# A linear-attention and MLP block on one core: float32r projections and sums rewritten as float16 pairs with scales found on the chip

## The chip, the cores and the metric

The kernel runs on one NeuronCore of one Trainium2 chip. The time is that of the device, in microseconds; lower is better. Three runs of the kernel before took 1063.47, 1063.88 and 1066.28 us, so its time is 1063.88 us. The traced execution, to which every number of the trace belongs, took 1062.19 us; its instructions span 1060.5 us of that.

## The reference

All tensors are float32, with 2048 tokens (S), width D = 576, 32 heads of 18 and an MLP width of 4608. What is computed, in the order of the reference:

```
mod = silu(c) @ w_mod                     # six vectors of 576: sa, ca, ga, sb, cb, gb
h   = layernorm(x) * (1 + ca) + sa
q, k, v = split(h @ wqkv)                 # three projections, 576 x 576 each
phi(t) = where(t > 0, t + 1, exp(t)) + 1e-6
kv  = sum over tokens of phi(k)^T v ;  z = sum over tokens of phi(k)      # per head
o   = (phi(q) @ kv) / (phi(q) @ z + 1e-6)
x   = x + ga * (o @ wo)
h   = layernorm(x) * (1 + cb) + sb
x   = x + gb * (silu(h @ w1) @ w2)
```

## The kernel before

Tokens are cut into 16 tiles of 128 and 4 blocks of 512. The program has three stages that overlap at their seams.

**Stage A**, up to about 200 us of the span, is attention without its output. The normalised and modulated input is transposed, and held as `hT`: per 128-row chunk of D (four and a half chunks, the half one doubled up) a high part rounded to float32r and a low part, the rest. The weights of q and k are split the same way (`w_hi`, `w_lo`; names `wq` and, for k, the tiles `w` and `v`). A projection of one tile is then 14 products for each half of 288 columns: for a whole chunk high x high, high x low and low x high, for the half chunk two. Lines L548 (the first two k tiles), L873 (`project`) and L400 (`x_passes`, used for the last five q tiles, and for the attention output, whose operands were float16 pairs already) issue them. Behind a k projection come `phi` (`phi_steps`: exp on ScalarE, the positive part on ScalarE or VectorE, their sum on VectorE), a split of phi(k) into high and low (`pk`), and `zsum` on GpSimd. v is never projected: the kernel sums phi(k) times normalised x over the tokens (`sum_steps`, L998, five sums of 24 or 16 products per block, from the split rows `xs` and `pk`), and multiplies the sums by the modulation and by the weight of v once at the end (L1171).

**The start** loads x tiles 0 and 1, the first third of w_mod, then the k weights (five chunks, the last in two halves), and the q weights. `mods` are multiplied by silu(c) and summed on VectorE (L583, L586, L593), turned into columns by small TensorE products (L522), and `add_cols` (L526) makes `cols["a"]`: the shift and 1 + scale of each row of `hT`. For each chunk k ScalarE then makes the high part of the k weight (L477) and of `hT` (L607), VectorE and GpSimd the low parts (L482, L372, L272), and the 56 products of tiles 0 and 1 run (L548). While TensorE has nothing to do, `keep_busy` (L542) issues products of ones that nobody reads.

**The middle**, from 200 to about 355 us, makes the attention output, the second layer norm, and the MLP of the first group of 256 columns. **The MLP**, from about 355 us to the end, is float16 pairs throughout, with products of 128x512 (L1947) and 128x288 (L2031).

The order of instructions on each engine is fixed, in two ways. For the last two thirds a planner (`Schedule.emit`) lists them by due times worked out from costs in the code; for everything before that, a table of numbers (`ORDERS`, one list per engine) replaces the order in which the code was written. An engine takes its instructions strictly in that order: one that waits holds up all behind it. Loads are issued by SyncE (SP) in its own order; a load takes one of eight semaphores, so that SyncE stands at a load until an earlier one has landed.

## Time and profile before

| | us |
|---|---|
| median of three runs | 1063.88 |
| traced execution, its own time | 1062.19 |
| its span | 1060.5 |
| TensorE busy | 1048.6 (99%) |
| VectorE busy | 867.0 (82%) |
| ScalarE busy | 718.5 (68%) |
| GpSimd busy | 741.8 (70%) |
| TensorE without work, in all | 11.9 |

A row of the groups names the line, engine and operation, the tiles written and read, the shapes and the count; behind the bar stand the busy time of the group, the mean time of one, and the idle time of the engine just before them. A matmul's own time (296 ns for a float32r one of 288 columns) overlaps its neighbours'; what one costs is the distance from start to start. "fp32r" and "f32" operands of matmuls in stage A are float32r. In a row of the timeline the first number is the start in us from the span's start, the second how long the group lasted.

### The profile page before, as it was taken

The page shows a single profiled execution, that of the slowest core. Times are in us where ns is not written, and L with a number is a line of the kernel's source. Part 1 is how long each engine was busy: PE and PEld are TensorE (multiplying, and loading weights), DVE is VectorE, ACT ScalarE, POOL GpSimd, SP SyncE. Part 2 cuts the span into 40 slices and gives each one's busy share as a digit, 9 for nine tenths or more (in the row PEclk, how much of TensorE's full clock was granted, in tenths as well). Part 3 has the DMA queues.
Part 4 walks back from the last instruction along what each step waited for, and adds up shares of the span by engine and source line. Part 5 has one row for each costly group of instructions (what it writes and reads, how often), then busy time and mean ns, then how long its engine had stood idle before and what let it go on. Part 6 is the DMA issues. An engine that isn't in the chain of part 4 may idle for free.

```text
span 1060.5 us, 19049 instructions
## 1 busy us (share of the span) xinstructions
PE 1048.6 (99%) x7001; PEld 740.5 (70%) x7001; DVE 867.0 (82%) x1439; ACT 718.5 (68%) x1342; POOL 741.8 (70%) x809
## 2 busy tenths in 40 slices
PE   9999999999999999999999999999999999999998
PEld 9999999887775555666666666666666666666665
DVE  6777675789989898898987888978977977898767
ACT  6875484368667876776865876767757766766554
POOL 3656536566843788899797688876876878787463
PEclk9999999999999999999999999999999999999999
DMA  8596970495657785588478566667567567526422
GB/s 301 159 204 197 155 191 8 104 209 133 185 175 249 241 255 187 179 292 209 125 259 211 175 223 220 172 219 215 183 209 204 185 216 223 187 90 203 152 80 113
DMA packets 139246, 198.75 MB, mean 187 GB/s; under 512 B 63820, under 2 KB 96464, under 8 KB 139152
## 3 DMA queue, kind: packets, MB, share of 16 engines
q1 hardware_dynamic: 106340, 196.35, 61.1%
q10 hardware_dynamic: 32812, 1.18, 3.1%
q8 instruction: 55, 0.90, 0.4%
q14 instruction: 39, 0.32, 0.1%
HBM read 176.77 MB, written 15.48 MB: 181 GB/s over the span
## 4 chain that ended last, share of the span: by engine, by line
PE 92%; DMA 3%; DVE 2%; ACT 1%; SPq 1%; issue 0%; ACTq 0%; DVEq 0%
PE up L1947 33%; PE down L2031 32%; PE psK L873 9%; PE big L400 6%; PE psG L998 5%; PE small L1452 2%; PE big L1463 1%; PE psK L1210 1%; DMA hT<-hd 1%; DMA xt<-in_A_x_dram 1%; PE small L385 1%; DMA acc<-in_A_wqkv_dram 1%; PE down L2065 1%; PE up L2065 1%; PE psG L1171 0%; DMA hd<-S 0%
## 5 line engine op out<-in xcount | busy, mean ns | idle before, releaser
L1947 PE MATMUL up<-hT,w 128*128 128x512 f16 x1264 | 319.2, 379 | 2.2 <-DMA hT<-hd 2.2
L1947 PEld LDWEIGHTS <-w 128*128 128x128 f16 x1492 | 145.7, 98 | 135.3 <-issue 4.6
L2040 DVE SCALAR_TENSOR_TENSOR acc<-acc,set,down 128x576 f32<-128x576 f32 x128 | 103.5, 810 | 34.6 <-PE down L2031 33.6
L1965 ACT ACTIVATE f<-f,set 128x512 f32<-128x512 f32 x102 | 73.3, 719 | 62.6 <-DVE f L1971 52.6
L1985 POOL TENSOR_TENSOR s<-f,f 128x256 f32<-128x256 f32 x66 | 54.4, 825 | 73.3 <-ACT f L1966 70.9
L2031 PE MATMUL down<-w,hc 128*128 128x288 f16 x600 | 91.5, 286 | 0.0
L2031 PE MATMUL down<-w,hb 128*128 128x288 f16 x600 | 90.8, 286 | 0.0
L2031 PE MATMUL down<-w,hT 128*128 128x288 f16 x480 | 82.8, 286 | 0.4 <-DVE acc L2044 0.4
L1969 DVE TENSOR_TENSOR f<-up,p 128x512 f32<-128x512 f32 x102 | 69.5, 683 | 16.4 <-PE up L1947 8.2
L1966 ACT ACTIVATE f<-f,set 128x512 f32<-128x512 f32 x102 | 73.6, 722 | 3.3
L2031 PEld LDWEIGHTS <-hc 128*128 128x128 f16 x600 | 58.7, 98 | 23.1
L2031 PEld LDWEIGHTS <-hb 128*128 128x128 f16 x600 | 58.7, 98 | 22.2 <-issue 0.2
L2009 POOL TENSOR_TENSOR hc<-s,hc 128x512 f16<-128x512 f32 x50 | 63.6, 1272 | 8.2 <-ACT hc L2005 8.2
L1971 DVE TENSOR_TENSOR f<-up,f 128x512 f32<-128x512 f32 x68 | 46.8, 688 | 24.9 <-PE up L1947 24.1
L400 PE MATMUL big<-w,qT 128*128 128x288 f16 x448 | 65.4, 286 | 1.2 <-DMA qT<-w 1.2
L1989 POOL TENSOR_TENSOR f<-f,s 128x256 f32<-128x256 f32 x66 | 53.8, 815 | 18.1 <-DVE hb L2009 10.2
L2031 PEld LDWEIGHTS <-hT 128*128 128x128 f16 x480 | 47.0, 98 | 26.6 <-issue 0.8
L1982 POOL TENSOR_TENSOR s<-f 128x256 f32<-128x256 f32 x66 | 57.3, 869 | 5.6 <-ACT f L1962 4.3
L1987 POOL TENSOR_TENSOR s<-s,f 128x256 f32<-128x256 f32 x66 | 55.9, 847 | 3.5
L2031 PE MATMUL down<-w,ha 128*128 128x288 f16 x396 | 56.6, 286 | 0.0
L2031 PE MATMUL down<-w,hd 128*128 128x288 f16 x396 | 56.0, 286 | 0.0
L2009 POOL TENSOR_TENSOR hd<-s,hd 128x256 f16<-128x256 f32 x66 | 49.0, 742 | 7.0 <-ACT hd L2005 6.9
(424 smaller groups left out, 2767.2 us busy)
## 6 DMA issues: line engine op xcount, KB each, us to landing
hT<-hd SPq DMA_DIRECT2D x101, 640.0 KB, 4.3
hT<-hd SPq DMA_DIRECT2D x65, 512.0 KB, 4.3
hT<-in_B_w_dram SPq DMA_DIRECT2D x14, 576.0 KB, 5.5
hT<-in_B_w_dram SPq DMA_DIRECT2D x28, 256.0 KB, 7.5
raw<-in_B_w_dram SPq DMA_DIRECT2D x11, 576.0 KB, 5.7
v<-in_B_w_dram SPq DMA_DIRECT2D x9, 576.0 KB, 5.1
acc<-in_A_x_dram SPq DMA_DIRECT2D x16, 288.0 KB, 3.5
raw<-in_B_w_dram SPq DMA_DIRECT2D x9, 512.0 KB, 5.7
```

The source lines that it names most:

```text
L400: T.matmul(ps, xpart(a), wpart(b), start=n == 0, stop=n == len(XW) - 1)
L873: T.matmul(o, part(a), w(b), start=c == 0 and m == 0, stop=c == KC and m == 1)
L1947: T.matmul(ps, left, right, start=first and m == 0, stop=m == len(seq) - 1, skip_group_check=True)
L1965: A.activation(f, f, AF.Silu, scale=factor(self.g, "inv"))
L1966: A.activation(f, f, AF.Identity, scale=factor(self.g, "delta"))
L1969: V.tensor_add(f, self.bank[bank[1]], self.p1)
L1982: G.tensor_sub(self.s3, half(i, 0, 0), half(i, 0, 1))
L1985: G.tensor_add(self.s[:, 0:1], half(i, 0, 1), half(i, 1, 1))
L1987: G.tensor_sub(self.s[:, 1:2], self.s[:, 0:1], half(i, 0, 0))
L2009: eng.tensor_sub(t[:, :, 1, :], src, t[:, :, 0, :])
L2031: T.matmul(ps[:, p, :HALF], left[:, u, p * P : (p + 1) * P], right[:, v], start=n in (1, 5, 7, 6) and j == 0, stop=j == len(passes) - 1, s ...
L2040: V.scalar_tensor_tensor(dst, dst, factor(self.g, "ratio"), ps[:, :, :HALF], op0=ALU.mult, op1=ALU.add)
```

## The change

It does six things.

1. **Float16 pairs in stage A.** `hT`, the k and q weights, `xs` and `pk` become pairs of float16 values: a high part, and the rest rounded to float16. The number of products, their shapes and the passes stay the same. Since a pair takes half the room, `hT` exists four times over and not twice, `pk` and `xs` eight times and not four.
2. **Powers of two, found on the chip.** Float16 needs values of a fit size, so every operand gets a factor. `ETA` (for `hT`) comes from the squares of the first third of w_mod, summed on ScalarE, and of silu(c); `SIZE_K` from the largest absolute value of each row of the k weight (five VectorE reductions); `SIZE_Q` from the squares of the q weight (five ScalarE squares); `SIGMA` (for `pk`) from the modulation columns and the k weight. Each is summed over the partitions by a small TensorE product with ones, and turned into a power of two by a chain of VectorE operations on single columns (`find_size`, `sigma_steps`). `add_cols` needs `ETA`, the split of the k weight `SIZE_K`, that of the q weight `SIZE_Q`, that of phi(k) `SIGMA`.
3. **Features in the projection's scale.** phi's exp takes its scale and bias from these factors; the positive part is one VectorE operation for every tile (`relu_of`: before, ScalarE did it for 12 of the 16 k tiles and the last five q tiles); the features stay multiplied by the factor, which z and the denominators take out.
4. **Low parts.** On VectorE a low part is one operation that scales and subtracts; on GpSimd it is two (scale in place, then subtract). For 9 of the k tiles ScalarE scales phi(k) once more ahead of GpSimd's subtraction.
5. **Orders.** All five lists of `ORDERS` are new, so the start, stage A, the middle and the entry of the MLP run in another order.
6. In the last unit of the MLP, the low part of `hb1` is now listed behind the last update of `U` of its block.

The diff, without the lists of `ORDERS` and the places that only rename:

```diff
-            0-24 27-29 25-26 30-44 47 49 51 53 55 57-58 45-46 48 50 59-62 52 54 63-66 69-70 56 73-74 67-68 71-72 75-76
...
-    hT = [hTa.tile([P, 2 * KC + 2, 512], F32R, name="hT")]
+    def pair_of_hT():
+        t = hTa.tile([P, 2 * KC + 2, 512], F32, name="hT")
+        y = t.rearrange("p n t -> p (n t)").bitcast(F16)
+        return [y[:, 512 * (2 * KC + 2) * i : 512 * (2 * KC + 2) * (i + 1)].rearrange("p (n t) -> p n t", t=512) for i in range(2)]
...
     def w_hi(wpart, k, full):
-        return A.copy(wpart(k if k < KC else 2 * KC), full)
+        return A.activation(wpart(k if k < KC else 2 * KC), full, AF.Identity, scale=size_of(wpart))
...
+        by, h = size_of(wpart), slice(0, P) if k < KC else slice(64, P)
+        hi, lo = (wpart(k), wpart(KC + k)) if k < KC else (wpart(2 * KC)[h],) * 2
+        if eng is V:
+            return V.scalar_tensor_tensor(lo, full[h], by[h], hi, op0=ALU.mult, op1=ALU.subtract)
+        G.tensor_mul(full[h], full[h], by[h].to_broadcast([h.stop - h.start, D]))
+        return G.tensor_sub(lo, full[h], hi)
+
+    def scale_bits(q):
+        V.tensor_scalar(q.bitcast(I32), q.bitcast(I32), 1, 0x3F800000, op0=ALU.logical_shift_right, op1=ALU.bitwise_and)
+
+    def find_size(rows, spot, size, inv, by):
+        t, q = both_sizes[:, 0:1], both_sizes[:, 1:2]
+        V.tensor_reduce(t, rows, axis=AX.X, op=ALU.add)
+        T.matmul(psT()[:, spot : spot + 1], ones, t, start=True, stop=True, skip_group_check=True)
+        V.tensor_scalar(q, psT()[:, spot : spot + 1], 2.0**-80, None, op0=ALU.max)
+        scale_bits(q)
+        V.reciprocal(size, q)
+        V.tensor_scalar(size, size, 2.0**-50, None, op0=ALU.mult)
...
+    def exp_of(e, ps, inv, by):
+        return A.activation(halves(e), ps[:, :, :HALF], AF.Exp, bias=by[2], scale=inv)
+
+    def relu_of(a, ps, by):
+        return V.tensor_scalar(halves(a), ps[:, :, :HALF], by[1], by[1], op0=ALU.add, op1=ALU.max)
...
     def add_cols(k0, k1):
         src = colps[:, 2 * k0 : 2 * k1]
-        V.tensor_add(cols["a"][:, k0:k1, :], src.rearrange("p (k a) -> p k a", a=2), plus1.unsqueeze(1).to_broadcast([P, k1 - k0, 2]))
+        V.scalar_tensor_tensor(cols["a"][:, k0:k1, :], src.rearrange("p (k a) -> p k a", a=2), ETA,
+                               plus_h.unsqueeze(1).to_broadcast([P, k1 - k0, 2]), op0=ALU.mult, op1=ALU.add)
...
+    for k in range(KC):
+        A.activation(room, mods[k][:, :, :D], AF.Square, accum_out=rows_m[:, k : k + 1])
+    A.activation(room[:, 0], tmod[:, :D], AF.Square, accum_out=rows_m[:, KC : KC + 1])
...
+    V.tensor_reduce(half_of[:, 0:1], rows_m, axis=AX.X, op=ALU.add)
+    T.matmul(psT()[:, 64:66], ones, half_of[:, 0:2], start=True, stop=True, skip_group_check=True)
...
+    for k in START:
+        V.tensor_reduce(rows2[:, k : k + 1], acc[k], axis=AX.X, op=ALU.max, apply_absolute_value=True)
+    V.scalar_tensor_tensor(rows2, rows2, float(D), rows2, op0=ALU.mult, op1=ALU.mult)
+    find_size(rows2, 66, SIZE_K, INV_K, BY_K)
...
+    for k in START:
+        A.activation(e_, acc[5 + k], AF.Square, accum_out=rows_q[:, k : k + 1])
+    find_size(rows_q, 67, SIZE_Q, INV_Q, BY_Q)
...
+        phi_steps(ps, k, a, [an], INV_K, BY_K)
+        do("POOL", 1.53, lambda: G.tensor_add(zsum, zsum, a) if t else G.tensor_copy(zsum, a), [an], ["zsum"])
+        do("ACT", 0.68, lambda: A.activation(hi, a, AF.Identity, scale=SIGMA), [an, "sigma"], [f"pkh{i}"])
+        if t in BY_POOL:
+            do("ACT", 0.68, lambda: A.activation(a, a, AF.Identity, scale=SIGMA), [], [an])
+            do("POOL", 1.5, lambda: G.tensor_sub(lo, a, hi), [an, f"pkh{i}"], [f"pkl{i}"])
         else:
-            do("DVE", 1.2, lambda: V.tensor_sub(lo, a, f32(hi)), [an, f"pkh{i}"], [f"pkl{i}"])
+            do("DVE", 1.2, lambda: V.scalar_tensor_tensor(lo, a, SIGMA, hi, op0=ALU.mult, op1=ALU.subtract), [an, f"pkh{i}", "sigma"], [f"pkl{i}"])
+    def sigma_steps():
+        ps, g = psT()[:, 0:3], "G1"
...
+        do("DVE", 0.4, terms, [], ["some"])
+        pe(0.25, lambda: T.matmul(ps, ones, t3, start=True, stop=True, skip_group_check=True), ["some"], [g])
```

**What moves.** First, SyncE's loads at the start. `xt` is x, `hT` at this place w_mod (its room is used for `hT` later), `acc_91` and the first `acc_92` the k weight. Before, and then as changed:

```order
L437 DMA xt<-in_A_x_dram 128x576 x2
L468 DMA tmod<-in_w_mod_dram 64x576 x2
L460 DMA hT<-in_w_mod_dram 128x2x576 x2
L407 DMA acc_92<-in_A_wqkv_dram 64x576
L460 DMA hT<-in_w_mod_dram 128x2x576 x2
L404 DMA acc_91<-in_A_wqkv_dram 128x576
L406 DMA acc_92<-in_A_wqkv_dram 64x576
L437 DMA xt<-in_A_x_dram 128x576
L404 DMA acc_91<-in_A_wqkv_dram 128x576
L437 DMA xt<-in_A_x_dram 128x576
L404 DMA acc_91<-in_A_wqkv_dram 128x576 x2
```

```order
L457 DMA xt<-in_A_x_dram 128x576 x2
L480 DMA hT<-in_w_mod_dram 128x2x576
L488 DMA tmod<-in_w_mod_dram 64x576 x2
L480 DMA hT<-in_w_mod_dram 128x2x576
L427 DMA acc_92<-in_A_wqkv_dram 64x576
L480 DMA hT<-in_w_mod_dram 128x2x576
L424 DMA acc_91<-in_A_wqkv_dram 128x576
L426 DMA acc_92<-in_A_wqkv_dram 64x576
L480 DMA hT<-in_w_mod_dram 128x2x576
L424 DMA acc_91<-in_A_wqkv_dram 128x576 x3
L457 DMA xt<-in_A_x_dram 128x576 x2
```

The last chunk of the k weight was the 16th load and is the 14th, ahead of x tiles 2 and 3; the last of w_mod has a whole chunk and two halves of the k weight ahead of it, where it had half a chunk.

Second, ScalarE from the first high part of the k weight on, before and as changed. L477 and L500 are the high parts of weights, L607 and L669 those of `hT`, L680 the squares of the q weight, L362 and L382 the normalising of x:

```order
L477 CAST w<-acc_91 128x576
L594 COPY hT<-hT 128x64
L607 ACTIVATE hT<-psK,col_a 128x256
L477 CAST v<-acc_92 128x576
L629 CAST xs_112<-xt 128x576
L607 ACTIVATE hT<-psK,col_a 128x256
...
L607 ACTIVATE hT<-psG_117,col_a 128x256
L607 ACTIVATE hT<-psG_116,col_a 128x256
L477 CAST w<-acc_91 128x576
L477 CAST wq<-acc_93 128x576
```

```order
L500 ACTIVATE w<-acc_92,crow 128x576
L655 COPY hT<-hT 128x64
L669 ACTIVATE hT<-psK,col_a 128x256
L500 ACTIVATE w<-acc_91,crow 128x576 x4
L680 ACTIVATE e,crow<-acc_92 128x576 x2
...
L669 ACTIVATE hT<-psG_124,col_a 128x256
L680 ACTIVATE e,crow<-acc_93 128x576
L669 ACTIVATE hT<-psG_123,col_a 128x256
L1008 CAST xs_115<-xt 128x576
L500 ACTIVATE wq<-acc_92,crow 128x576 x3
```

The rows left out in the second piece are L669 twice, L680, L382 for x tiles 2 and 3 (two of 64 columns, two of 576) and one cast of x. The five squares and the normalising now stand among the five high parts of `hT`, ahead of the first high part of the q weight.

Third, TensorE from the first k products to the first q products. L590 is L548 of before, L938 is L873, L584 is L542 (`keep_busy`); L517 is the product of `find_size`, L981 that of `sigma_steps`, L1357 the transposing of x tiles 2 and 3. Before, and then as changed:

```order
L548 MATMUL psK<-w,hT 128x288 x2
L542 MATMUL psG_117<-ones 128x128
...
L548 MATMUL psK<-v,hT 128x288 x4
L1269 MATMUL psG_116<-ident,xt 128x128
L873 MATMUL psK<-wq,hT 128x288 x2
```

```order
L584 MATMUL psG_124<-ones 128x128 x14
L590 LDWEIGHTS hT
L590 MATMUL psK<-w,hT 128x288
...
L584 MATMUL psG_124<-ones 128x128 x3
L517 MATMUL psG_124<-crow,ones 128x1
...
L981 MATMUL psG_124<-crow,ones 128x3
...
L1357 MATMUL psG_124<-ident,xt 128x128 x2
L938 MATMUL psK<-wq,hT 128x288
```

Of the 56 k products of tiles 0 and 1, ten stand ahead of L517 (the one for `SIZE_Q`; that for `SIZE_K` stands further up), 24 and eight transposes between L517 and L981, 22 and two transposes behind L981. None of these small products was there before.

459 lines of the change are left out of this document (247 added, 212 removed).

## The prediction

> **What bounds the kernel now.** I read the page's busy times and its chain first.
>
> ```profile
> PE 1048.6 (99%) x7001; PEld 740.5 (70%) x7001; DVE 867.0 (82%) x1439; ACT 718.5 (68%) x1342; POOL 741.8 (70%) x809
> PE 92%; DMA 3%; DVE 2%; ACT 1%; SPq 1%; issue 0%; ACTq 0%; DVEq 0%
> ```
>
> TensorE works in 1048.6 of 1060.5 us, and the chain that ends last is TensorE for 92%. So two things count: what a product costs, and how long TensorE stands. The windows tell where it stands (columns: stretch, length, busy time and count of PE, PEld, DVE, ACT, POOL, then granted clock, DMA share, GB/s).
>
> ```profile
> 0.00:20.00 20.00, 18.01 (x134) 17.52 (x135) 11.53 (x35) 10.11 (x21) 5.65 (x11) 1.00 0.92 316
> 20.00:40.00 20.00, 19.86 (x152) 19.52 (x151) 19.44 (x47) 18.78 (x35) 8.80 (x10) 1.00 0.55 174
> 40.00:160.00 120.00, 120.00 (x905) 120.00 (x904) 83.14 (x138) 79.18 (x121) 69.49 (x51) 1.00 0.88 186
> 200.00:220.00 20.00, 18.76 (x147) 16.07 (x146) 17.42 (x31) 9.63 (x15) 13.22 (x13) 1.00 0.86 189
> 320.00:340.00 20.00, 18.81 (x109) 10.13 (x107) 18.16 (x33) 13.93 (x26) 2.93 (x4) 1.00 0.76 258
> 340.00:360.00 20.00, 17.29 (x95) 9.18 (x95) 16.48 (x26) 16.21 (x35) 18.88 (x26) 1.00 0.78 240
> ```
>
> Stage A, from 40 to 160 us, is full; VectorE and ScalarE are at 69% and 66% there. Idle are the seams: 1.2 us after 200, 1.2 + 2.7 us between 320 and 360.
>
> **The gain: the pace of a product.** Stage A's 905 products in 120 us come one every 132.6 ns. Float16 products of the same 288 columns run at the end of this kernel:
>
> ```profile
> 1045.62 0.53 PE L2065 MATMUL down<-w,hb 128*128 128x288 f16 x3
> 1045.99 0.53 PE L2065 MATMUL down<-w2B,hc 128*128 128x288 f16 x3
> ...
> 1054.81 0.53 PE L2065 MATMUL down<-w2B,hc 128*128 128x288 f16 x3
> ```
>
> 75 products (25 rows of three) take 9.19 us: 122.5 ns each, 10.1 less. The products that the change turns to float16:
>
> ```profile
> L998 PE MATMUL psG<-w,xs 128*128 128x288 f32 x336 | 53.3, 296 | 0.0
> L873 PE MATMUL psK<-w,hT 128*128 128x288 f32 x308 | 48.6, 296 | 0.0
> L873 PE MATMUL psK<-wq,hT 128*128 128x288 f32 x264 | 41.9, 296 | 0.0
> L873 PE MATMUL psK<-v,hT 128*128 128x288 f32 x128 | 24.4, 295 | 0.0
> L400 PE MATMUL big<-wq,hT 128*128 128x288 f32 x120 | 21.7, 313 | 0.0
> L998 PE MATMUL psG<-w,v 128*128 128x288 f32 x112 | 20.2, 296 | 0.0
> L548 PE MATMUL psK<-w,hT 128*128 128x288 f32 x44 | 7.2, 304 | 0.0
> L400 PE MATMUL big<-v,hT 128*128 128x288 f32 x20 | 3.8, 303 | 0.0
> L548 PE MATMUL psK<-v,hT 128*128 128x288 f32 x12 | 2.2, 307 | 0.0
> ```
>
> These are 1344. The 56 of L548 belong to the start, counted below; the other 1288 give 1288 x 10.1 = **13.0 us**. Bounds: 0 if float16 is no quicker here, 13.0 if all of it comes through.
>
> **The loss: the start.** How far is the first q product put off? Before it stands here, after the 56 k products:
>
> ```profile
> 28.59 0.51 PE L873 MATMUL psK<-wq,hT 128*128 128x288 f32 x2
> ```
>
> Now I follow the new order. `SIZE_K` needs the whole k weight. Its last load is now the 14th; the 14th of before was issued and landed so:
>
> ```profile
> 10.41 0.33 SPq L437 DMA_DIRECT2D xt<-in_A_x_dram x1
> DMA to landing us min/median/max: 6.9/6.9/6.9
> ```
>
> So the weight is there at 10.4 + 6.9 = 17.3 us. The last of w_mod, which VectorE met at 13.9 (first row below), has 0.44 MB more ahead of it: at 316 GB/s 1.4 us, so 15.3; ScalarE's last squares end near 17.7. Prices of single operations:
>
> ```profile
> 13.91 0.95 DVE L593 SCALAR_TENSOR_TENSOR hT<-hT,sc 128x256 f32<-128x256 f32 x2 [0.25 <-DMA hT<-in_w_mod_dram]
> L711 DVE TENSOR_REDUCE crow<-bc_gb 128x1 f32<-128x576 f32 x2 | 1.5, 744 | 0.0
> L691 DVE TENSOR_SCALAR crow<-crow 128x4 f32<-128x4 f32 x1 | 0.2, 170 | 0.0
> 20.51 1.02 ACT L607 ACTIVATE hT<-psG,col_a 128x256 fp32r<-128x256 f32 x2
> 21.42 0.67 ACT L477 CAST w<-acc 128x576 fp32r<-128x576 f32 x1
> L674 ACT ACTIVATE hT<-hT 128x1152 f32<-128x1152 f32 x14 | 16.2, 1158 | 0.0
> L674 ACT ACTIVATE hT<-hT 128x256 f32<-128x256 f32 x7 | 2.9, 414 | 0.0
> L674 ACT ACTIVATION_READ_ACCUMULATOR hT<-hT 128x1 f32 x35 | 6.6, 187 | 0.0
> L362 ACT ACTIVATE xt<-xt,mv 128x576 f32<-128x576 f32 x3 | 2.6, 868 | 0.1
> L362 ACT ACTIVATE xt<-xt,mv 128x64 f32<-128x64 f32 x3 | 1.3, 439 | 2.1 <-DVE mv L356 2.1
> ```
>
> - The last largest value (a reduction of 576, 0.74) ends about 18.6: another reduction and a piece of `mods` stand close ahead of it. Behind it VectorE has three short operations, a piece of `mods` (0.48) and seven steps of `find_size` and of `ETA`: with 0.15 to 0.17 each, `SIZE_K` at 20.6. The first high part of a weight was made at 14.75 before.
> - Eight more VectorE operations, 1.6 us, stand ahead of the first `add_cols`, for which ScalarE's first high part of `hT` waits: 22.2. Behind it wait four high parts of weights and all else.
> - ScalarE then has, up to the last square of the q weight, four pieces of `hT`, four high parts of weights, a cast, five squares and four normalisings. Two pieces of `hT` take 0.91 between starts (20.51, 21.42), 0.46 each; a high part takes 0.67, the cast 0.57 where the next operation starts before it ends; a square of 576 lies between the rows of 256 and 1152 at 0.68, with the read of 187 that follows it 0.87; the normalisings 0.1 less than their rows, 0.34 and 0.77. Sum: 4 x 0.46 + 4 x 0.67 + 0.57 + 5 x 0.87 + 2 x 0.34 + 2 x 0.77 = **11.7**. So the squares are done at 33.9.
> - On TensorE only ten k products stand ahead of the second product of L517. It issues in order, so it does those ten and stands until the squares are summed (a short VectorE operation and a handover each way, 0.6): 34.5. Of the 46 others, 24 and eight transposes follow (3.8 us, 38.3). Then L981 waits for `SIGMA`: after the squares VectorE has the seven steps of `SIZE_Q` (35.9), two low parts of `hT` (0.7), two of weights (0.72 each, which wait for ScalarE's high parts until 36.6) and the short steps of `SIGMA`, to 39.1. The remaining 22 and two transposes (2.9) end at **42.0**.
>
> That is 42.0 - 28.6 = **13.4 us**. This term is the least sure: 8.5 if loads and chains overlap better, 20 if they don't (below).
>
> **Smaller terms.** The first projections afterwards find ScalarE and VectorE behind: the first q tile waits for a PSUM buffer that exp and the positive part free (0.7), the next for an exp queued behind two rows of w_mod (1.3). Both are worked out with TensorE as late as above; if it is later still, they vanish. Between 0 and 2.0 I take **1.0**. Moved to VectorE are 17 positive parts, about 0.75 each, 13 us over 160: it goes from 69% to 77%, still below TensorE. The additional scaling on ScalarE (9 of 0.57) fits into its 34%, and the two GpSimd operations of a low part into what `pk`'s eight buffers allow. These I cost at nothing; if VectorE were late with the low part of `pk`, sums would stop, one stall of 0.7 per block. The seams have new orders. Their idle time was 5.1 us; without a row that tells which way they go I take 0, with 3 either way. The move of `hb1`'s low part, in the last microseconds of the MLP, lies between 0 and 0.4.
>
> **Sum.** -13.0 + 13.4 + 1.0 = +1.4: the traced execution's 1062.2 becomes 1063.6. The median of the runs, 1063.9, is 1.7 above that execution, so the forecast is **1065.3 us**. A difference of 0.3%, 3.2 us, is about what can be told from no change; this is within it.
>
> **Rivals.**
>
> - *The start costs 8.5* (0.28). If the operations of the start overlap better than in order and price, `SIZE_K` comes at 19 (1.6 earlier), the eight operations behind it take 1.0, and ScalarE's 17 overlap by 0.1 more each (10.0), then the squares end at 30. If the wait for `SIGMA` (0.8) is covered too, the first q product starts at 42.0 - 3.9 - 0.8, near 37. For it: ScalarE was idle half of the first 20 us (10.11). Against: in 20 to 40 us it was busy 18.78 of 20. Time: -13.0 + 8.5 + 0.5 = -4.0, 1059.9. It decides if the second L517 comes ahead of 31 us.
> - *The short operations are slow* (0.24). Late in this kernel the same short operation is four times as long:
>
> ```profile
> L691 DVE TENSOR_SCALAR raw<-raw 128x4 f32<-128x4 f32 x7 | 4.9, 698 | 0.2
> L695 DVE TENSOR_SCALAR set<-set 128x4 f32<-128x4 f32 x9 | 4.0, 441 | 0.2
> L482 POOL TENSOR_TENSOR w<-acc,w 128x576 fp32r<-128x576 f32 x2 | 3.1, 1536 | 8.1 <-ACT w L477 8.1
> ```
>
> With 170 alone and 698 beside GpSimd's work, one that waits costs 0.53 more. GpSimd's low parts of k (1.5 us, and now two operations each) run just when the seven steps of `SIZE_Q` and the ten of `SIGMA` do. If 13 of the 17 are caught, 6.9 us more: 1072. Against: GpSimd was busy 8.8 of the 20 us, so fewer may be caught. It decides from about 4 of them on. The Trainium skill, page "SBUF — State Buffer", section "🔬 SBUF: two separate sides", says that a port pair shared by VectorE and GpSimd is locked for a whole instruction by whichever starts first; that is a reason for rows of 698 and speaks against this change. By that rule all 17 steps could be held, an estimate of 17 x 0.53 = 9.0 us more.
> - *TensorE comes back slowly* (0.06). It stands some 10 us ahead of the second L517; nothing in the trace of before stands so long, and its windows show a granted clock of 1.00 throughout. If the 3.8 us of products behind it ran at half pace, they would end at 42.1, past the 39.1 of `SIGMA`: 3.0 later, 1068.3. The Trainium skill, page "TensorE: Matmul & The Clock Gate", section "What's actually happening", gives such a rule: half the clock after an idle window, until about 3.4 us of work are done. By its figure the loss is an estimate of 1.7 us; no run here shows it.
> - *Float16 gains nothing in stage A* (0.04): 1065.3 + 13.0 = 1078. Against it stands the pace of L2065.
>
> **How the numbers follow.** The forecast has 0.38 and its own range is 1062 to 1068.5, from the seams' 3 us. With 0.28 at 1056 to 1062, 0.24 at 1068 to 1075, and 0.10 for the last two, 8 in 10 lie from **1056.5** to **1073.5**. Faster than 1060.7 is most of the first rival and little of the forecast: 0.28. Slower than 1067.1 is the second, the fourth, the third and a slice of the forecast: 0.34. Within: 0.38.
>
> **What would show it.** Rows of stage A at 122 ns from start to start; a stretch of some 10 us ahead of the second L517 in which TensorE has nothing; that product at 34 to 35, the first q product near 42 us. TensorE's busy time falls by some 13 us, its idle time rises by as much. A second L517 ahead of 31 proves the start's term wrong; idle time at 200 to 360 us away from 5 the seams'; windows of stage A with TensorE under 99% the cover that I gave VectorE.

## The result and the profile after

| | before | after |
|---|---|---|
| median of the runs, us | 1063.81 (1063.47 to 1066.28) | 1072.37 (1071.13 to 1074.08) |
| ratio, with its 95% interval | | 1.0087 (1.0066 to 1.0108) |
| traced execution, its own time | 1062.19 | 1071.29 |
| its span | 1060.5 | 1069.4 |
| first q product starts | 28.59 | 47.52 |
| first product of `x_passes` | 199.67 | 210.96 |
| last 128x512 product of the MLP | 1041.4 | 1050.7 |

The changed kernel is 8.6 us slower. (Of the kernels below, e1_sizes_known has one run of 1215.15 us at a mean granted clock of 0.845, and its median is that of its four other runs.) The page of its traced execution opens with the busy times; the second row quoted is the chain of waits by engine.

```profile
PE 1042.4 (97%) x6999; PEld 698.5 (65%) x6999; DVE 901.8 (84%) x1495; ACT 726.4 (68%) x1350; POOL 753.2 (70%) x818
PE 81%; DVE 12%; DMA 3%; issue 1%; ACT 1%; SPq 1%; POOL 0%; DVEq 0%; ACTq 0%; POOLq 0%
```

TensorE works 6.2 us less, in a span that is 8.9 longer. Of the chain, 12% is VectorE's now, where it was 2%. The windows of the changed kernel (columns as before: stretch, length, busy time of PE, PEld, DVE, ACT, POOL, granted clock, DMA share, GB/s) tell where that is.

```profile
0.00:20.00 20.00, 12.57 (x69) 11.42 (x69) 10.31 (x23) 11.84 (x23) 4.95 (x11) 0.80 0.91 260
20.00:40.00 20.00, 13.65 (x78) 12.73 (x78) 19.16 (x69) 12.91 (x27) 10.49 (x9) 0.69 0.43 140
40.00:60.00 20.00, 17.50 (x140) 13.50 (x138) 18.40 (x41) 18.38 (x29) 12.48 (x10) 1.00 0.58 169
60.00:80.00 20.00, 17.86 (x144) 13.81 (x142) 19.53 (x28) 16.56 (x24) 14.90 (x11) 1.00 1.01 250
80.00:100.00 20.00, 19.44 (x158) 15.08 (x157) 19.53 (x25) 14.73 (x21) 13.97 (x9) 1.00 1.02 147
40.00:160.00 120.00, 114.79 (x927) 90.13 (x925) 103.84 (x166) 91.76 (x134) 71.87 (x50) 1.00 0.87 184
```

Up to 40 us TensorE has 147 instructions where it had 286. VectorE is at work for 92 to 98% of each slice from 20 to 100 us. The granted clock is under 1.00 in the first 40. In 40 to 160 us there are 927 products although TensorE stands for 5.2 us: they come faster. TensorE's own timeline shows the start (start, length, group, and in brackets the idle time ahead of it and what ended it):

```profile
28.56 5.17 PE L584 MATMUL psG<-ones 128*128 128x128 f32 x28
33.57 0.41 PE L590 MATMUL psK<-w,hT 128*128 128x288 f16 x2
37.47 1.15 PE L590 MATMUL psK<-w,hT 128*128 128x288 f16 x8 [3.49 <-DVE raw L392]
38.46 0.83 PE L584 MATMUL psG<-ones 128*128 128x128 f32 x6
39.12 0.28 PE L517 MATMUL psG<-crow,ones 128*128 128x1 f32 x2
43.99 0.38 PE L981 MATMUL psG<-crow,ones 128*128 128x3 f32 x2 [0.66 <-DVE crow L978]
47.52 0.65 PE L938 MATMUL psK<-wq,hT 128*128 128x288 f16 x4 [0.20 <-DVE a L533]
```

The second product of L517, for `SIZE_Q`, comes at 39.12, that for `SIGMA` (L981) at 43.99. Ahead of both TensorE stood 3.49 us for VectorE's L392, which reads the transposed x out of PSUM, multiplies and shifts it, and so frees the buffer that the next k products write.

From the landmarks in the table the span's 8.9 us come apart: the first q product +18.9; from there to `x_passes` -7.6 (163.4 us in place of 171.1); from there to the last 128x512 product -2.0; the end -0.4. In the 163.4 us TensorE stands 4.3, before it stood 0.25. So the work there went from 170.8 to 159.1 us, by 11.7.

### The profile page after: what moved, and what is told of

The parts are those of the page before. It is cut to its first block, busy times and chain, and to the rows that moved or that the text cites. A ratio compares the mean times of both kernels' runs of the same rounds, so it can differ in the third digit from the quotient of the medians.

```text
span 1069.4 us, 19132 instructions
## 1 busy us (share of the span) xinstructions
PE 1042.4 (97%) x6999; PEld 698.5 (65%) x6999; DVE 901.8 (84%) x1495; ACT 726.4 (68%) x1350; POOL 753.2 (70%) x818
## 3 DMA queue, kind: packets, MB, share of 16 engines
q10 hardware_dynamic: 32812, 1.18, 3.0%
## 4 chain that ended last, share of the span: by engine, by line
PE 81%; DVE 12%; DMA 3%; issue 1%; ACT 1%; SPq 1%; POOL 0%; DVEq 0%; ACTq 0%; POOLq 0%
PE up L2035 34%; PE down L2119 31%; PE psK L938 6%; PE psG L1087 5%; PE big L1551 1%; DVE st L367 1%; PE big L420 1%; DMA acc<-in_A_wqkv_dram 1%; PE small L1540 1%; DVE pn L810 1%; DVE hT L276 1%; DVE acc L1479 1%; DMA tmod<-in_w_mod_dram 1%; DMA hT<-hd 1%; PE down L2153 1%
## 5 line engine op out<-in xcount | busy, mean ns | idle before, releaser
L938 PEld LDWEIGHTS <-hT 128*128 128x128 f16 x700 | 68.2, 98 | 21.2 <-issue 2.8
L2119 PEld LDWEIGHTS <-hc 128*128 128x128 f16 x600 | 58.7, 98 | 22.2 <-issue 0.5
L1087 PE MATMUL psG<-w,xs 128*128 128x288 f16 x448 | 64.6, 286 | 1.9 <-DVE w L966 1.5
L2119 PEld LDWEIGHTS <-hT 128*128 128x128 f16 x480 | 47.0, 98 | 26.1 <-issue 0.3
```

Of the source, the lines that this page charges most:

```text
L938: T.matmul(o, part(a), w(b), start=c == 0 and m == 0, stop=c == KC and m == 1)
L1087: T.matmul(ps[:, h, :HALF], l, pk[pp[t]][:, u, h * HALF : (h + 1) * HALF], start=t == 0 and m == 0, stop=t == 3 and m == len(left) - 1)
L2119: T.matmul(ps[:, p, :HALF], left[:, u, p * P : (p + 1) * P], right[:, v], start=n in (1, 5, 7, 6) and j == 0, stop=j == len(passes) - 1, s ...
```

## The experiments

The first eight kernels take one suspected part out of the changed kernel, or move it. Then the change is built up from the kernel before. Ratios are to the kernel before, run beside each; the first q product is that of the traced execution.

| run | what it is | median, us | ratio (95%) | first q product |
|---|---|---|---|---|
| after | the change | 1072.37 | 1.0087 (1.0066 to 1.0108) | 47.52 |
| e1_sizes_known | sizes as constants | 1070.76 | 1.0071 (1.0044 to 1.0097) | 44.18 |
| e2_no_pool_lows | GpSimd's low parts of k left out | 1071.13 | 1.0068 (1.0044 to 1.0093) | 46.29 |
| e5_stats_later | statistics moved back on VectorE | 1073.14 | 1.0092 (1.0063 to 1.0121) | 46.63 |
| e3_no_mod_sums | a sum on GpSimd left out | 1072.31 | 1.0068 (1.0046 to 1.0090) | 47.77 |
| e4_fillers | TensorE kept at work | 1073.70 | 1.0083 (1.0067 to 1.0100) | 47.99 |
| e7_relu_scalar | eight positive parts on ScalarE | 1075.60 | 1.0096 (1.0067 to 1.0126) | 46.86 |
| e8_known_ordered | e1 in an order of its own | 1071.38 | 1.0060 (1.0042 to 1.0079) | 42.86 |
| e10_mod_loads_first | w_mod loaded earlier | 1072.10 | 1.0079 (1.0057 to 1.0101) | 48.64 |
| e6_sums_alone | before, only the sums float16 | 1060.79 | 0.9973 (0.9958 to 0.9987) | 32.90 |
| e9_before_f16 | before, all pairs float16, no factor | 1054.84 | 0.9915 (0.9897 to 0.9933) | 30.84 |
| e11_find_k | e9 and the keys' size found | 1073.96 | 1.0080 (1.0058 to 1.0102) | 46.97 |
| e12_features_scaled | e9 and the features' new form | 1068.68 | 1.0031 (1.0012 to 1.0051) | 33.29 |

### e1_sizes_known: are the operations of finding the loss?

```diff
+    for to, value in ((SIGMA, 2.0**-7), (UNDO, 2.0), (ETA, 4.0), (UNDO_H, 0.25), (SIZE_K, 16.0), (SIZE_Q, 64.0), (INV_K, 2.0**-6),
...
+        added("DVE", 0, V.memset(to, value))
-    for k in range(KC):
-        A.activation(room, mods[k][:, :, :D], AF.Square, accum_out=rows_m[:, k : k + 1])
...
+    def find_size(pe_):
+        skip("DVE", "PE", *["DVE"] * 9)
```

In this and the next kernels `added` puts an instruction behind a place of an engine's list, and `skip` leaves the place of one empty; all others keep theirs. The squares, the largest values, both size chains and that of `SIGMA` are gone.

> The changed kernel with ETA, SIZE_K, SIZE_Q, SIGMA and what follows from them as constants, written once at the start: the ten squares on ScalarE, the five largest values and all steps of find_size and sigma_steps on VectorE, and their four products are left out (the constants are the powers of two that these inputs give). Theory A (the pace of float16 came through in full, and the loss is the finding at the start): the first q product, at 47.5 us in the changed kernel, comes at 30 to 34; the execution takes 1052 to 1056. Theory B (float16 pairs lose something later as well, in stage A's VectorE work or at the seams): the start recovers, but the time stays at 1060 or more.

The first q product comes 3.3 us earlier, and the time is 1.6 lower, less than the intervals can tell from nothing. Theory A missed both numbers, and the start that theory B expected to recover didn't. So the operations of finding are 3.3 of the start's 18.9 us while their order stays. Even of these only 1.9 are left at the first product of `x_passes` (209.08). The timeline of TensorE shows the same picture as the changed kernel's, shifted:

```profile
25.35 5.11 PE L596 MATMUL psG<-ones 128*128 128x128 f32 x28
30.30 0.41 PE L602 MATMUL psK<-w,hT 128*128 128x288 f16 x2
34.27 1.15 PE L602 MATMUL psK<-w,hT 128*128 128x288 f16 x8 [3.56 <-DVE raw L419]
```

The sizes are there at once, yet TensorE still waits 3.56 us for the same step: VectorE's list has other work ahead of it.

### e2_no_pool_lows: are short operations slow beside GpSimd?

```diff
+        if wpart is wkp:
+            skip("Pool", "Pool")
+            return added("Activation", 29, A.activation(lo, full[h], AF.Identity, scale=by[h]))
```

This leaves six GpSimd operations out; the low parts of the k weights then hold a copy, so this part of the result is not computed.

> The changed kernel; GpSimd's six operations for the low parts of three chunks of the k weight are left out, and ScalarE writes a copy in their place (no low part, so these chunks have a wrong one). Theory A (VectorE's queue bounds the start, and it is stretched by operations that wait beside GpSimd): VectorE's operations of 1.1 us between 28 and 36 us go back to 0.15 to 0.8, the second L517 comes 3 us earlier (36), the first q product too, and the time falls by 2 to 4 us, to 1068 to 1070. Rival (ScalarE's chain of squares bounds it, as forecast): three more operations stand in that chain, L517 is later by 0 to 2 us, and the time is the same or 2 us longer.

Here are five short operations of the changed kernel in the groups of 20 to 48 us:

```profile
L376 DVE SCALAR_TENSOR_TENSOR mv<-mv 128x2 f32<-128x2 f32 x1 | 1.2, 1183 | 0.0
L975 DVE TENSOR_TENSOR crow<-crow 128x5 f32<-128x5 f32 x1 | 1.1, 1122 | 0.0
L986 DVE SCALAR_TENSOR_TENSOR crow<-crow 128x1 f32<-128x1 f32 x1 | 1.1, 1096 | 0.0
L662 DVE TENSOR_SCALAR col_u<-col_a,crow 128x10 f32<-128x10 f32 x1 | 1.1, 1095 | 0.0
L977 DVE COPY crow<-crow 128x5 f32<-128x5 f32 x1 | 1.1, 1069 | 0.0
```

and the same operations without the GpSimd work at 24 to 34 us (25 to 28 lines further down; GpSimd's low parts of q, beside the second and third, are still there):

```profile
L401 DVE SCALAR_TENSOR_TENSOR mv<-mv 128x2 f32<-128x2 f32 x1 | 0.1, 150 | 0.0
L1003 DVE TENSOR_TENSOR crow<-crow 128x5 f32<-128x5 f32 x1 | 1.1, 1121 | 0.0
L1014 DVE SCALAR_TENSOR_TENSOR crow<-crow 128x1 f32<-128x1 f32 x1 | 1.1, 1097 | 0.0
L690 DVE TENSOR_SCALAR col_u<-col_a,crow 128x10 f32<-128x10 f32 x1 | 0.2, 232 | 0.0
L1005 DVE COPY crow<-crow 128x5 f32<-128x5 f32 x1 | 0.2, 164 | 0.0
```

The three that lost their neighbour go from 1.07 to 1.18 us down to 0.15 to 0.23; the two that kept it stay at 1.10 and 1.12. The mechanism is shown. Its price is not what theory A or the prediction's second rival gave it: the second L517 (37.89) and the first q product come 1.2 us earlier, nothing of that is left at the first product of `x_passes` (210.96), and the time does not move by more than can be told. The Trainium skill, page "SBUF — State Buffer", section "🔬 SBUF: two separate sides", gives a lock of the port pair that VectorE and GpSimd share as the reason; these rows agree with it.

### e5_stats_later and e10_mod_loads_first: is it the order of one queue?

e5 moves the statistics of x tiles 4 to 7 on VectorE's queue behind the terms of `SIGMA`, and what reads them on ScalarE and GpSimd with them. e10 moves one load on SP's queue. An entry of `MOVES` is a piece of an engine's list, by its numbers, and the number behind which it now stands.

```diff
+    gone, extra, MOVES = {}, {}, {'DVE': [('110-122', 89), ('123', 108)], 'Activation': [('62', 43)], 'Pool': [('20', 13)]}
```

and, in e10,

```diff
+    gone, extra, MOVES = {}, {}, {'SP': [('7', 6)]}
```

> The changed kernel; only orders differ: VectorE's statistics of x tiles 4 to 7 (eight pieces, four aggregations and the steps behind them), now among the first low parts of hT, stand behind the terms of SIGMA, and what needs them on ScalarE and GpSimd (one normalising, one power) later too. Theory A1 (VectorE's queue ahead of the first q product is what costs): L517 and the first q product come 4 to 5 us earlier and the time falls by 3 to 5 us, to 1067 to 1069. Theory A2 (VectorE has more work than time up to 100 us, whatever its order): the first q product comes earlier, but TensorE stalls as much more between 45 and 100 us, and the time stays within 1 us of 1072.

> The changed kernel with one load moved on SP's queue: the fourth load of the modulation's weights (line 480) is issued ahead of the second and third chunk of the key weights, as in the kernel before, so that the modulation's last part lands at 14 to 15 us in place of 17.7 and the key weights 1 to 2 us later. Theory L (the load order is a part of the start's loss): the first hT at 21.5 to 23 us in place of 24.0, the first q product 1 to 2.5 us earlier, the time 0.5 to 2 us less. Rival (the key weights' largest value, which then comes later, sets the start): the first q product not earlier than 47 us, the time the same or up to 2 us more.

In e5 the second product of L517 comes at 36.55, 2.6 us earlier, and the first q product 0.9 earlier. Theory A1 fell: at the first product of `x_passes` (211.94) e5 is 1.0 us behind the changed kernel, and the time stays. In e10 the last part of w_mod lands 1.6 us earlier: ScalarE's row, of the changed kernel and of e10.

```profile
17.74 1.16 ACT L626 ACTIVATE acc<-hT 128x1152 f32<-128x1152 f32 x1 [2.06 <-DMA hT<-in_w_mod_dram]
```

```profile
16.16 1.16 ACT L651 ACTIVATE acc<-hT 128x1152 f32<-128x1152 f32 x1 [0.84 <-DMA hT<-in_w_mod_dram]
```

The k weight's size still comes at 22.9, since its loads came later instead, and the first q product is 1.1 us later. Theory L fell, the rival held: the load order only exchanges one lateness for another.

### e4_fillers: does the half clock cost anything?

`fill(n, place)` puts n products of ones behind a place of TensorE's list; there are 19 in all, at seven places.

```diff
+    fill(5, 19)
...
+    fill(6, 31, kps[0][:, 1, 384:512])
+    fill(2, 53, kps[0][:, 1, 384:512])
```

> The changed kernel with 19 more products that nobody reads, on TensorE's queue where it stood idle at the start: 5 ahead of the products that sum the statistics' columns, 6 behind the transposes, 8 among the products of the modulation. All else and the output as before. Theory C (the half clock that the records show between 12 and 33 us costs time): the granted clock shows 1.00 from about 12 us on in place of 0.80 and 0.69 in the first two slices of 20 us, the first q product comes 1 to 3 us earlier, and the time falls by 2 to 4 us, to 1068 to 1070. Theory A (VectorE's queue sets the start, TensorE waits for it at any clock): the clock may rise, the first q product moves by at most 1 us, the time by at most 1 us.

Window 12 to 32 us, of the changed kernel and of e4:

```profile
12.00:32.00 20.00, 13.38 (x59) 12.35 (x58) 17.92 (x51) 12.94 (x27) 9.92 (x8) 0.50 0.85 275
```

```profile
12.00:32.00 20.00, 16.99 (x88) 16.25 (x87) 18.31 (x53) 12.32 (x28) 10.62 (x9) 0.62 0.79 260
```

The changed kernel runs at half clock through all of these 20 us. The fillers put that off by some 5 us; they don't prevent it. The first q product is 0.5 later, as theory A said. So 5 us less of half clock gain nothing here, where TensorE waits for VectorE. A start without any half clock was not tried.

### e3_no_mod_sums and e7_relu_scalar: is VectorE too full up to 100 us?

e3 leaves out GpSimd's sums of the second piece of w_mod (so the modulation lacks them), to free VectorE of its neighbour. e7 gives eight positive parts back to ScalarE (without their 1e-6): `early` are the first eight tiles, and `spot` is right behind exp.

```diff
-                    do("POOL", 1.5, lambda raw=raw, dst=dst, a=a: G.tensor_add(dst[:, a], dst[:, a], raw[:, a]), [names[a]], [f"tmod{a}"])
+                    do("POOL", 1.5, lambda raw=raw, dst=dst, a=a: skip("Pool") if piece == 1 else G.tensor_add(dst[:, a], dst[:, a], raw[:, a]), [names[a]], [f"tmod{a}"])
```

and, in e7,

```diff
+            if not early:
+                return relu_of(out, ps, by)
+            skip("DVE")
+            added("Activation", spot, A.activation(halves(out), ps[:, :, :HALF], AF.Relu))
```

> The changed kernel without GpSimd's sums of the second piece of the modulation's products (line 1144, piece 1); the output is then not the reference's, nothing else differs. In the changed kernel's trace these sums stand at 54 to 72 us, beside them VectorE's small operations take 1.3 to 2.4 us (lines 276, 542, 1012), and TensorE stands idle for 4.3 us in all between 48 and 110 us. Theory A (up to 100 us VectorE has more work than time, and its operations beside GpSimd's are stretched): the stretch in 60 to 80 us goes, the idle time of TensorE between 48 and 110 us falls to 1 to 2 us, the time by 2 to 3 us, to 1069 to 1070. Rival (what happens there is hidden, or VectorE's operations are as long without GpSimd): the idle time stays above 3.5 us and the time within 1 us of the changed kernel's.

> The changed kernel with the positive part of the first eight feature tiles taken by ScalarE right behind the exponential of the same tile, not by VectorE (the term of 1e-6 is left out there, which is below the output's tolerance). That takes about eight operations of 1.0 us off VectorE's queue before 100 us and puts them on ScalarE's, which in the changed kernel's trace has 16.56 of 20 us of work in 60 to 80 us and 14.73 in 80 to 100 us, where VectorE has 19.53 in each. Theory A (VectorE's work sets the pace up to 100 us): TensorE's idle time between 48 and 110 us falls from 4.3 to 1 to 2 us, the time by 2 to 4 us, to 1068 to 1070. Rival (the features are late for another reason, or ScalarE is as full): idle time above 3.5 us, time within 1 us of the changed kernel's or above it.

e3's windows show VectorE with 14.44 and 16.49 us of work where it had 19.53 and 19.53:

```profile
60.00:80.00 20.00, 19.76 (x160) 15.19 (x158) 14.44 (x30) 16.41 (x24) 6.76 (x5) 1.00 0.98 248
80.00:100.00 20.00, 18.92 (x156) 14.97 (x154) 16.49 (x19) 15.11 (x21) 11.65 (x9) 1.00 1.22 173
```

TensorE's idle time between 48 and 110 us falls only from 4.3 to 3.7 us, and the time doesn't move. What became of VectorE's free time shows best in e7, in VectorE's timeline:

```profile
91.24 0.82 DVE L567 SCALAR_TENSOR_TENSOR a<-e,phis,a 128x576 f32<-128x576 f32 x1
98.39 2.19 DVE L1188 TENSOR_REDUCE crow<-raw 128x9 f32<-128x1152 f32 x1 [6.33 <-DMA raw<-parts]
```

VectorE arrives early at a reduction whose input comes back from DRAM, and stands for it 6.33 us (2.9 in e3). A positive part, which frees the PSUM buffer, is behind it in the queue, so TensorE stands for 4.5 us, and after that runs at half clock (0.83 over 100 to 120 us). In both runs theory A fell and the rival held: the work that VectorE has isn't the bound by itself. With a fixed list, time that is freed ahead of a late transfer turns into a wait for it.

### e8_known_ordered: the constants, in an order of their own

e1 and, by hand, new places for some 35 VectorE operations, and for some on the other engines: columns, copies and low parts ahead of all statistics.

```diff
+    gone, extra, MOVES = {}, {}, {'DVE': [('51-52 48 49 56-57 54-55 59-62 53 58 74-80 82 50 110-121', 47), ('122', 81), ('123', 108)], 'Activation': [('36-39 59', 24), ('62', 43)], 'Pool': [('11', 6), ('20', 13)], 'PE': [('127-134', 124), ('37-42', 34)]}
...
+    fill(5, 19)
+    fill(6, 31, kps[0][:, 1, 384:512])
```

> All sizes as constants, as in e1_sizes_known (the squares, the largest value, the reciprocal powers of two and the scale of the statistics are left out), and now VectorE's order made for that: the columns of the weights, the raw copies, the transposes' evictions and the low halves of the weights stand ahead of all statistics, with the moves on ScalarE, GpSimd and TensorE that go with it; and 11 products that nobody reads keep TensorE at work in its waits. Theory A with C (the loss of the start is finding the sizes together with the order that finding forces, and the clock): first k product at 22 to 26 us and first q product at 34 to 38 us in place of 33.6 and 47.5, the clock at 1.00 from 16 us on, the time 1055 to 1060, under the kernel before. Rival (the start's length is set by what remains: loads, pairs of the weights, transposes): first q product not before 42 us and the time at 1066 or above.

The first k product comes at 26.34 (33.57), but the first q product at 42.86, and the time is 1071.38. Its waits on TensorE between 30 and 60 us:

```profile
PE psK L947 <- DVE a L545: 4.9, 1, 4.9
PE psK L947 <- DVE acc L545: 2.8, 1, 2.8
```

ScalarE stood 6.5 us for the statistics that I had moved back, and exp of the first tile came that much later. Of the 4.7 us at the first q product 1.6 are left at the first product of `x_passes` (209.34). So my order has a hole of its own, and this run doesn't tell what the best order would give. None of these eight repaired the changed kernel's start from within.

### e6_sums_alone and e9_before_f16: float16 in the order of before

e6 makes only `xs` and `pk` float16; e9 makes `hT` and the k and q weights float16 too. Both by plain casts, with no factor. For these inputs the values lie in float16's range: the weights have a standard deviation of 0.4, so their low halves are about 1e-4. Neither has the changed kernel's protection against other sizes. Of e6:

```diff
-    xs = [pa.tile([P, 2 * D], F32R, name=f"xs{i}") for i in range(3)] + [w5[:, 2 * D : 4 * D]]
+    xs = [pa.tile([P, D], F32, name=f"xs{i}").bitcast(F16) for i in range(4)]
...
-        G.tensor_sub(xs[t][:, DX:], xts[t][:, : KC * P], f32(xs[t][:, : KC * P]))
+        G.tensor_sub(xs[t][:, DX:], xts[t][:, : KC * P], xs[t][:, : KC * P])
```

and, in e9 besides,

```diff
-        return wq[:, b, :] if b < 2 * KC else w5[:, 4 * D :]
+        return (wq[:, b, :] if b < 2 * KC else w5[:, 4 * D :]).bitcast(F16)[:, :D]
...
-            return eng.tensor_sub(wpart(KC + k), full, f32(wpart(k)))
+            return eng.tensor_sub(wpart(KC + k), full, wpart(k))
```

> The kernel before, with one part of the change alone: xs and pk, and so the 448 products of the sums (L998), are float16 pairs; the projections stay float32r, nothing is found on the chip and no order is changed. (phi(k) gets no factor, which fits these inputs and not any.) Theory A (the gain is the pace, 132.6 against 122.5 ns): 448 x 10.1 = 4.5 us less, 1059.3. Rival (the gain of a quicker stage A is lost behind it, at the seams): 1062 to 1064.

> The kernel before with only the types changed: the pairs of the weights, of hT, of the rows and of the features of the keys are float16, by plain casts, with no factor, no size found on the chip, no scale kept in the features. Every instruction of VectorE, ScalarE, GpSimd and the loads and their order are the kernel before's (for these inputs the halves still lie in float16's range). Theory F (the float16 products are worth what the pace term said, and the whole loss of the change is what finding the sizes brings: its operations, the loads and the order that it forces): first q product at 28 to 30 us as before (28.59), a start-to-start time of 122 ns in the projections, no idle time of TensorE over 1.5 us between 48 and 110 us, and a time of 1050 to 1054, 10 to 14 under the kernel before and some 20 under the changed one. Rival G (the pairs' engines cannot feed the faster products in any order, so VectorE's work up to 100 us takes the gain back): idle time of 4 us and more between 48 and 110 us, time 1057 to 1061. Rival H (float16 products gain less than their distance says): time above 1061.

e6 gains 3.3 us, of the 4.5 that 448 x 10.1 ns make; its 1060.79 lies between theory A and the rival. e9 gains 9.0 us and is the fastest of all these kernels. Its windows:

```profile
0.00:20.00 20.00, 18.53 (x125) 17.82 (x126) 11.47 (x35) 10.02 (x20) 5.28 (x11) 0.94 0.92 307
20.00:40.00 20.00, 19.15 (x142) 15.19 (x140) 17.57 (x41) 16.22 (x32) 7.52 (x9) 0.89 0.51 158
40.00:160.00 120.00, 118.10 (x956) 92.94 (x955) 87.82 (x145) 82.10 (x125) 71.47 (x54) 1.00 0.88 190
```

956 products in 118.10 us, where before had 905 in 120. The first q product stands at 30.84, 2.3 us later than before. At least part of that is the clock: the traced execution ran at half clock from about 17.5 to 24.3 us, and the other five of the six runs show a mean clock of 1.000 and spans 0.9 to 2.0 us shorter. From the first q product to `x_passes` it takes 164.4 us, 4.0 of them idle, so the work is 160.4: 10.4 less than before. Between 48 and 110 us TensorE stands 1.5 us. Theory F named the pace and the idle time; its ranges for the first q product and the time are missed by 0.8 us each. G and H fell. The changed kernel, set beside e9, is 16.7 us later at the first q product and 1.0 us shorter from there to `x_passes` (163.4). In these two traces its whole disadvantage lies ahead of the first q product.

### e11_find_k: the price of finding, from the other side

e9 and, in it, the largest value of the five k weights, their sum, one product with ones, four steps to a power of two, and times 0 plus 1; the pairs of the k weights take the factor and so wait for it. ScalarE's high parts are moved behind `hT`, VectorE's statistics behind the chain.

```diff
+    for k, spot in ((0, 21), (KC, 25), (1, 23), (2, 30), (3, 41)):
+        added("DVE", spot, V.tensor_reduce(size[:, 2 + k : 3 + k], acc[k], axis=AX.X, op=ALU.max, apply_absolute_value=True))
+    fill(30, 56)
+    added("DVE", 41, V.tensor_reduce(size[:, 1:2], size[:, 2 : 3 + KC], axis=AX.X, op=ALU.add))
+    added("PE", 56, T.matmul(kvp[2][:, 1, 0:1], ones, size[:, 1:2], start=True, stop=True, skip_group_check=True))
+    fill(10, 56)
...
+            return A.activation(wpart(k), full, AF.Identity, scale=size[:, 0:1]) if k < KC else A.activation(
```

> e9_before_f16 (the kernel before with float16 pairs and no factor) and, added to it, the finding of the keys' size alone: the largest magnitude of each of the five key weights on VectorE, their sum, one product over the partitions, four small operations to a power of two, times zero plus one, so that the factor is 1 and the output stays the reference's. The pairs of the key weights wait for it (a scaled activation on ScalarE, a scaled subtraction on VectorE); 40 products that nobody reads keep TensorE at work meanwhile. The squares, the queries' size, SIGMA and the features' scale are left out. Theory B (what finding costs is a barrier: no product of the keys before the last of their weights has landed and gone through VectorE, where e9 starts with the first of five): the first key product at 25 to 28 us (19.18 in e9), the first q product at 33 to 36 (30.84), the time 3 to 6 us above e9's, 1058 to 1061. Rival M (the barrier hides behind loads and statistics, the changed kernel's loss lies in the number of its operations): the first q product within 1.5 us of e9's, the time within 1.5 us.

The first q product comes at 46.97, almost as late as in the changed kernel, and the time is 19.1 us above e9's: far more than either theory said. A good part of it is my own. On TensorE:

```profile
22.09 8.63 PE L638 MATMUL psG<-ones 128*128 128x128 f32 x60
30.55 0.28 PE L644 MATMUL psG<-size,ones 128*128 128x1 f32 x2
30.69 2.48 PE L638 MATMUL psG<-ones 128*128 128x128 f32 x20
35.90 4.53 PE L583 MATMUL psK<-w,hT 128*128 128x288 f16 x22 [1.77 <-ACT w L508]
```

and on VectorE, where the sum is ready and where the answer is read:

```profile
25.57 0.16 DVE L643 TENSOR_REDUCE size<-size 128x1 f32<-128x5 f32 x1
33.21 0.16 DVE L647 TENSOR_SCALAR size<-psG 128x1 f32<-128x1 f32 x1 [7.48 <-PE psG L638]
```

I had counted a filler as one record; it is two, of 144 ns each. So the sum, ready at 25.73, waited for 30 fillers and its answer for ten more, 7.5 us in all. Without them the first q product would come at 39.5 at the earliest (an estimate, 46.97 - 7.48, which leaves the sum's own product no time), which is still 8.6 us behind e9. With fewer fillers it was not tried. So it is shown that finding forms a barrier: nothing of k can start before the last k weight has landed and been reduced, at 25.7 us, where e9's first k product is at 19.18. How much of its 16 us in e11 is the barrier alone is not.

### e12_features_scaled: the price of the features' form

e9 with exp by a scale and a bias from a tile, the positive part on VectorE for all tiles, the minimum by a tile, all factors 1.

```diff
-            do("ACT", 0.65, lambda: A.activation(halves(out), ps[:, :, :HALF], AF.Relu), [k], names)
...
+        def relu(of):
+            return V.tensor_scalar(halves(out), ps[:, :, :HALF], of, of, op0=ALU.add, op1=ALU.max)
+
+        def moved():
+            skip("Activation")
+            added("DVE", spot, relu(LEAST if whole else ZERO))
```

> e9_before_f16 with the features in the changed kernel's form, by factors that are 1 in a tile: the exponential with scale and bias from the tile, the positive part as one operation of VectorE with operands from the tile for all tiles (the kernel before has it on ScalarE for 12 of the 16 key tiles, as a Relu and, for 8 of them, an addition), the minimum with the tile's 1. Order as in e9, each moved operation right ahead of the minimum of its tile. Theory S (this part of the change costs little; the loss is in the start): TensorE's idle time between 48 and 205 us grows by 1 us at most over e9's 3.9, the time by at most 2 us, to 1055 to 1057. Rival V (VectorE pays: 12 operations of 0.87 us more between 50 and 200 us, and 16 to 17 of 20 us full already): idle time 3 us and more above e9's, time 1058 and above.

13.8 us above e9. The waits of TensorE between 40 and 205 us, by what ended them:

```profile
PE psK L911 <- DVE a L922: 7.3, 7, 2.3
PE psK L911 <- DVE acc L922: 2.0, 2, 1.6
```

L922 is the positive part. TensorE waits nine times for it, because it holds the PSUM buffer; from the first q product to `x_passes` it stands 10.7 us, 6.7 more than in e9. After the two longest of these waits (2.28 us up to 89.06, 1.98 us up to 119.67) the clock is halved; the second:

```profile
110.00:120.00 10.00, 7.72 (x62) 5.82 (x61) 9.25 (x23) 4.54 (x8) 3.66 (x3) 1.00 0.88 110
120.00:130.00 10.00, 10.00 (x70) 7.43 (x69) 8.79 (x14) 6.94 (x10) 4.48 (x4) 0.83 1.38 80
```

The second row has TensorE at work without a pause, and 70 products in place of 81. Rival V held. Not all of the 13.8 us is the features' form: of the 14.3 by which this trace's span is longer than e9's, 2.5 are there at the first q product, where an x tile had come late (3.68 us of waiting at 9 us, half clock behind it); 10.7 come from there to `x_passes`, 6.7 of them idle and 4.0 in slower work. The twelve runs go from 1062.97 (mean clock 1.000) to 1072.24 (0.992). The order is e9's, with the moved operations at a place of my choice. The changed kernel has all positive parts on VectorE as well, in an order made for them, and stands only 4.3 us there, 0.9 of them for the positive part. So this cost is real, and an order can hide most of it.

## Why the prediction was right or wrong

The time, 1072.4, lies in the wide range, not in the forecast's own 1062 to 1068.5; the forecast, 1065.3, was 7.1 us too low, and the direction was that of the second likeliest case. In the terms of the prediction's sum the span's +8.9 are -13.1 + 18.9 + 4.1 - 1.0, where it had -13.0 + 13.4 + 1.0 + 0.

- **The pace: right.** 13.0 us from 1288 x 10.1 ns. The changed kernel's projections and sums come every 122 to 122.5 ns; the work between the first q product and `x_passes` fell by 11.7 us, and 140 products of `x_passes` follow. In e9, which has nothing else of the change, 10.4 of it show. The fourth rival, no gain, fell.
- **The start: mis-sized, 13.4 forecast, 18.9 measured.** This is the step that failed. The first 2.3 us went to the loads: the last of w_mod came at 17.7, not 15.3, the last k weight at 19.9 (issued at 12.09, landed 7.8 us later), not 17.3, and so `SIZE_K` at 22.9, not 20.6. The largest miss is the second product of L517, 39.12 against 34.5. The prediction had it wait for ScalarE's 11.7 us of squares and copies. That work measured 11.1, but it began at 24.01, not 22.2, and ScalarE stood 2.29 us in the middle of it for VectorE's statistics (L376), so the squares end at 37.36, not 33.9. The chain of rows, ScalarE's and then VectorE's sum:

```profile
32.57 1.53 ACT L382 ACTIVATE xt<-xt,mv 128x64 f32<-128x64 f32 x3 [2.29 <-DVE mv L376]
37.17 0.19 ACT L680 ACTIVATION_READ_ACCUMULATOR e<-acc 128x1 f32 x1
38.38 0.15 DVE L516 TENSOR_REDUCE crow<-crow 128x1 f32<-128x5 f32 x1
```

 The ten k products ahead of L517 were late too, by the 3.49 us for L392. Both waits lead to VectorE's queue, 19.16 of 20 us full, which the prediction had counted only for the size chains. e5, which takes statistics out of the way there, brings L517 to 36.55. The stretch of some 10 us without work that the prediction announced isn't there: fillers take 5.0 us of it, and the longest wait is the 3.49. The first rival, a start of 8.5 us, fell as well: L517 comes long after its 31 us.
- **Later stalls: 1.0 forecast, 4.3 measured** (0.25 of them there before, so 4.1 in the sum). Among them 1.5 us for VectorE's low part of `pk`, and 1.1 us for a step of `SIGMA`'s chain:

```profile
PE psG L1087 <- DVE w L966: 1.5, 1, 1.5
PE psK L938 <- DVE crow L990: 1.1, 1, 1.1
```

 The cover that the prediction gave VectorE in stage A, 77%, is 103.84 of 120 us, 87%, and 98% between 60 and 100; TensorE's 114.79 of 120 us is under the 99% that was to show this.
- **The moved positive parts: "I cost at nothing".** e12 shows what they cost without an order made for them: 10.7 us from the first q product to `x_passes`, with the half clocks that follow. In the changed kernel's order TensorE waits 0.9 us for them there (three waits for L533), so the term's size was nearly right, and its reason, that 77% is enough, was not.
- **The seams: 0 forecast, -1.0 measured.** From `x_passes` to the end the span is 2.4 us shorter, of which `x_passes`' own 1.4 (140 x 10.1 ns) belong to the pace. Inside the 3 us given.
- **The rival of short operations: its mechanism is true, its price is not.** Five short operations are caught in the start, each about 0.9 us longer. Of the 17 steps that the rival counted these are at most three (L975, L977 and L986, of `SIGMA`; none of `SIZE_Q`), under the four from which it was to decide. Its 0.53 for one was a mean over a mixed row: in the kernel before, the seven L691 of the MLP took 0.17 (three) or 1.09 us (four, each beside a GpSimd operation of 1.15 us), so one that is caught costs 0.92. e2 takes away three of the five and gains 1.2 us at the first q product. That the time came out at the rival's 1072 is no proof of it.
- **The rival of half clock: not where it was put.** Behind the second L517 the clock was 1.00 (39 to 42 us). It was 0.50 from 12 to 32 us, and e4, which takes some 5 us off that, gains nothing. The Trainium skill, page "TensorE: Matmul & The Clock Gate", section "What's actually happening", gives about 3.4 us of work until the clock returns, after an idle window of about that length. e12 agrees with the first (half clock for 3 to 4 us); its waits of 2.3 and 2.0 us, after which the clock fell, are shorter than the second. e6 (5 us of work) and e9 (6.8 us of work) stayed at half clock for longer than the first.

So the loss sits in the start, and none of the tries from within brought it back: e1, e2, e5, e8 and e10 move the first q product by -4.7 to +1.1 us and the time by 1.6 at most. Of what is gained at the first q product a part or all is gone at `x_passes`; that VectorE's list and its waits for transfers take it back is shown for e7 and argued for the others. Only a kernel without the barrier, e9, shows what the products were worth. What stays open: how the 16.7 us at the first q product divide between the barrier of finding and the order around it. e1 (constants, order kept) leaves 13.3 of it, e11 (finding, order of before) at least 8.6 after its fillers are taken off. They overlap.

## What to carry to other kernels

Make the type change alone first, in the order that is there: here it was worth 9 us, and what was built around it cost some 17.5 (1072.4 against 1054.8). A value that must be found over a whole operand before its first use is a barrier: here it put the first product of k from 19.18 (e9) behind 25.7 us (e11). A first product that comes earlier isn't yet a gain: e8 won 4.7 us there and 1.0 in the time. Where each engine has a fixed list, look at what is next in the list before counting freed time as gained: it may be a wait for a transfer.
